# Second-layer preparation moved to earlier tiles, its first unit dealt over the last tile, and the output scatters of the first chunk sent one per unit

## The chip, the cores and the metric

The kernel runs on one NeuronCore of a Trainium2 chip. A core has a matrix engine (TensorE, PE in the profile, its weight loads PEld), a vector engine (DVE), an activation engine (ScalarE, ACT), a general engine (GpSimd, POOL) and a queue engine (SyncE, SP) that here only issues DMAs. Each engine runs its own list of instructions in the order in which the program wrote it; semaphores order the engines against each other. The metric is the time of one execution in microseconds of the device, from start to end.

## The reference, cut to what matters

Three stages over N = 1152 tokens of width 512: attention with 8 heads of 64 (half of the heads with a local window of 32, half with a stride of 32), a routed layer (each token goes to the one of eight experts that its gate picks), and a dense layer (each token goes through all four experts, weighted by given shares).

```
x = attention(q, k, v)                                # [1152, 512]
e_idx = argmax(x @ w_gate + modality_bias[modality])  # first layer: 8 experts, width 1024
y[mask] = gate_w[mask] * (relu(x[mask] @ w1[e]) @ w2[e])
out += p[:, e] * (relu(y @ w1b[e]) @ w2b[e])          # second layer: 4 experts, width 1024
```

All of it is in float32. The kernel makes each float32 product from three passes: an operand is split into a high part (a rounded copy, made by ACT) and a low part (the difference, made by DVE or POOL), and TensorE adds high by high, high by low and low by high.

## The kernel before

The schedule is written out by hand; the order in which the Python code calls the helpers is the order of each engine's list.

**Attention and routing** take the first 100 us or so and are not touched.

**First layer** (`moe1`, 11 tiles of 128 tokens that share an expert). It is a software pipeline over k = 0 to 11: iteration k does the first product of tile k (`mm1`, lines 1016) between the transposes of tile k-1's hidden values (`htr`, line 1023) and then the second product of tile k-1 (`mm2`, lines 1037 to 1039, four steps u = 0 to 3 of six matmuls). The iteration that multiplies tile t for the second time is thus k = t + 1. The 512 KB weight blocks come through SP into eight buffers `raw` and are split by `W.ahead`, ACT making `wh` (line 844) and DVE `wl` (line 845). After step u the function `mid` is called, and after the tile `after`; they are `first_layer_mid(t, u)` and `first_layer_start(t)`. In the last iteration, k = n = 11, there is no tile left for a first product, and `before_last` puts the products of the second layer's first unit in its place.

**Preparing the second layer's tokens.** `places()` works out, in five steps of a few small DVE instructions, where each token lies. `x2_gather(j)` is an indirect DMA from POOL's queue that fetches block j of 128 tokens (line 1095). `x2_prep(j)` has two steps: the first transposes the block on TensorE (line 1128), copies it back (ACT, line 1130), forms four sums on POOL (lines 1134 to 1137) and splits three quarters (ACT line 1141, POOL line 1142); the second splits the four sums (the same two lines, 512 wide). The table `PREP` says after which (t, u) a step is called; u = 4 stands for the call in `after`. Four blocks, the first chunk of 512 tokens, are prepared within the first layer; the five others later.

**Second layer** (`m2_unit`, 32 units: two chunks of tokens, four experts, four quarters of the width). One unit makes seven products of six matmuls each (lines 1261 to 1263) in three PSUM banks X, Y and Z, from sums of quarters in the manner of Strassen. Bank X is used four times in a row and ACT or DVE reads it in between (`hidden`, and the copies of lines 1287, 1294, 1299). Between the products the second products of the unit before are woven in (`m2_mm2`, lines 1413 to 1416). The weights of a unit come from `Pieces`, a generator of five pieces a unit: `a` (768 columns), two of `w` and two of `s` (512 columns each). Each is split by ACT (line 1180) and DVE (line 1181) when `PC.put` or `hidden` asks for it. The two `s` pieces hold sums of weights that POOL forms in place after the `a` piece has been split:

```
nc.gpsimd.tensor_tensor(a22, a22, a21, op=ALU.add)        # 1201
nc.gpsimd.tensor_tensor(a21, a11, a21, op=ALU.subtract)   # 1202
nc.gpsimd.tensor_tensor(a11, a22, a11, op=ALU.subtract)   # 1203
nc.gpsimd.tensor_tensor(a12, a12, a11, op=ALU.subtract)   # 1204
```

**Output.** When the last expert has been added to a block of 128 rows (line 1426), `scatter(j)` sends the rows to their places in the output with an indirect DMA from POOL's queue (line 1431). There are four in the first chunk, all in unit 16, and five in the second chunk, at the very end.

Of the kernel before, what the change touches and what calls it, by code (L numbers as in the profile page):

```python
# [111 lines left out]
def fused_kernel(  # L112
# [486 lines left out]
    def with_rows(y, idx, n=NTOK):  # L599

        nc.gpsimd.indirect_dma_start(  # L601
            out=y[:, DM:], out_offset=None, in_=xx[:n, :], in_offset=bass.IndirectOffsetOnAxis(ap=idx, axis=0)
        )
# [244 lines left out]
    def m1_gather(t, pool):  # L848
        g = pool.tile([P, XW], F32, name="g")
        nc.gpsimd.indirect_dma_start(  # L850
            out=g[:, :DM], out_offset=None, in_=xe, in_offset=bass.IndirectOffsetOnAxis(ap=idx16[:, t : t + 1], axis=0)
        )
        return g
# [142 lines left out]
    def moe1(mp, tiles, W, gs, pool, mid, after, before_last):  # L996
        n = len(tiles)
        xs, hs, ys = {}, {}, {}

        def xprep(k):  # L1000
            g = gs.pop(k)
            y = mp.tile([P, XW], F32, name="y", bufs=3)
            with_rows(y, idx16[:, tiles[k] : tiles[k] + 1])
            xs[k] = x_parts(g) if k else x0
            ys[k] = y
            if k + 2 < n:
                gs[k + 2] = m1_gather(tiles[k + 2], pool)

        def mm1(k, ph, kc):
            xh, xl = xs[k]  # L1010
            key = "1", tiles[k], kc
            wh, wl = W.out.pop(key)
            s = slice(P * kc, P * (kc + 1))
            for xx, ww, first, last in ((xh, wh, kc == 0, False), (xh, wl, False, False), (xl, wh, False, kc == KC - 1)):
                for i in range(2):
                    nc.tensor.matmul(ph[i], xx[:, s], ww[:, 512 * i : 512 * (i + 1)], start=first, stop=last)
            W.release(key)

        def htr(k, i, ht):
            pt = pst.tile([P, 512], F32, name="ps_a")  # L1020
            for c in range(4):
                s = slice(512 * i + P * c, 512 * i + P * (c + 1))
                nc.tensor.transpose(pt[:, P * c : P * (c + 1)], hs[k][:, s], ident)
            hh = mp.tile([P, 512], F32R, name="hh")
            hl = mp.tile([P, 512], F32R, name="hl")
            split(hh, hl, pt)
            ht.append((hh, hl))

        def mm2(k, ht, py, u):
            key = "2", tiles[k], u  # L1030
            wh, wl = W.out.pop(key)
            for i in range(2):
                kc = 2 * u + i
                hh, hl = ht[kc // 4]
                s = slice(P * (kc % 4), P * (kc % 4 + 1))
                f = slice(512 * i, 512 * (i + 1))
                nc.tensor.matmul(py, hh[:, s], wh[:, f], start=(kc == 0), stop=False)
                nc.tensor.matmul(py, hh[:, s], wl[:, f], start=False, stop=False)
                nc.tensor.matmul(py, hl[:, s], wh[:, f], start=False, stop=(kc == FC - 1))
            W.release(key)  # L1040

        xprep(0)
        xprep(1)
        W.ahead()
        for k in range(n + 1):
            ht = []
            if k == n:
                before_last(W, 0)
            if k < n:
                ph = [psb.tile([P, 512], F32, name="ps_b") for _ in range(2)]  # L1050
                mm1(k, ph, 0)
            if k > 0:
                htr(k - 1, 0, ht)
            W.ahead()
            if k == n:
                before_last(W, 1)
            if k < n:
                mm1(k, ph, 1)
            if k > 0:
                htr(k - 1, 1, ht)  # L1060
            W.ahead()
            if k < n:
                mm1(k, ph, 2)
                if 0 < k < n - 1:
                    xprep(k + 1)
                W.ahead()
                mm1(k, ph, 3)
                h = mp.tile([P, FF], F32, name="h")
                for i in range(2):
                    nc.scalar.activation(h[:, 512 * i : 512 * (i + 1)], ph[i], AF.Relu)  # L1070
                hs[k] = h
                W.ahead()
            if k > 0:
                py = psb.tile([P, 512], F32, name="ps_b")
                for u in range(4):
                    mm2(k - 1, ht, py, u)
                    if k == n and u < 2:
                        before_last(W, 2 + u)
                    mid(tiles[k - 1], u)
                    if u < 3:  # L1080
                        W.ahead()
                y = ys.pop(k - 1)
                nc.scalar.activation(y[:, :DM], py, AF.Copy, scale=y[:, DM : DM + 1])  # L1083
                t = tiles[k - 1]
                nc.scalar.dma_start(out=ye[(t + 1) * P : (t + 2) * P, :], in_=y)
                W.ahead()
                after(t)
# [231 lines left out]
    place = places()  # L1319
# [1 line left out]
    first, prep = {}, {}  # L1321

    def first_layer_start(t):
        if t >= 3:
            next(place, None)
        for j in {5: (0, 1), 6: (2,), 7: (3,)}.get(t, ()):
            x2_gather(j)
        prep_step(t, 4)


    PREP = {(6, 2): 0, (7, 0): 0, (7, 1): 1, (7, 4): 1, (8, 0): 2, (8, 3): 2, (8, 4): 3, (9, 0): 3}

    def prep_step(t, u):
        j = PREP.get((t, u))
        if j is not None:
# [2 lines left out]
            PC.put((u + 1) // 2)  # L1338

    def first_layer_mid(t, u):  # L1340
        if t >= 3 and u == 1:
            next(place, None)
        prep_step(t, u)

# [7 lines left out]
    def second_layer_start(W, n):  # L1352

        if n == 0:
            m2_bank.extend(psb.tile([P, 512], F32, name="ps_b") for _ in range(3))
            first["u"] = m2_unit(0, first_tmp)
            PC.put(2)
        for _ in range((2, 2, 1, 2)[n]):
            next(first["u"])


# [40 lines left out]
    for q in range(2):  # L1402
        t = xh2.rearrange("p q c t -> p (q c t)"), xl2.rearrange("p q c t -> p (q c t)")
        HT.append([x[:, NH * q : NH * (q + 1)].rearrange("p (f t h o) -> p f t h o", f=2, h=2, o=HP) for x in t])

    def m2_mm2(u, i, fh, cols=slice(0, DM)):

        c, e, fb = units2[u]
        hh, hl = (h[:, fh, i].rearrange("p h o -> p (h o)") for h in h_of(u))
        wh, wl = (w[:, 512 * fh : 512 * (fh + 1)][:, cols] for w in WT["w", u])  # L1410
        po = m2_acc[i][:, cols]
        part = (c, e, i) == (1, E2 - 1, CHT[1] - 1)
        nc.tensor.matmul(po, hh, wh, start=(fb == 0 and fh == 1), stop=False, skip_group_check=part)  # L1413
        nc.tensor.matmul(po, hh, wl, start=False, stop=False, skip_group_check=part)  # L1414
        last = fb == FC // 2 - 1 and fh == 0
        nc.tensor.matmul(po, hl, wh, start=False, stop=last, skip_group_check=part)  # L1416
        if last:
            j = CH0[c] + i
            if e == 0:
                rows[j] = raws[KC + i // 2][:, DM * (i % 2) : DM * (i % 2 + 1)]  # L1420
            pe = ext2[:, j, 1 + e : 2 + e]
            row = rows[j][:, cols]
            if e == 0:
                nc.vector.tensor_scalar(row, po, pe, None, op0=ALU.mult)
            else:
                nc.vector.scalar_tensor_tensor(row, po, pe, row, op0=ALU.mult, op1=ALU.add)  # L1426
            if e == E2 - 1 and cols.stop == DM:
                scatter(j)

    def scatter(j):  # L1430
        nc.gpsimd.indirect_dma_start(  # L1431
            out=out,
            out_offset=bass.IndirectOffsetOnAxis(ap=oid[:, j : j + 1], axis=0),
            in_=rows[j],
            in_offset=None,
        )

    def second_groups(u):
        return [(u, i, fh) for fh in (1, 0) for i in range(CHT[units2[u][0]])]
# [4 lines left out]
        return raws[RAW - 1][:, HX * "abd".index(k) :][:, :HX]  # L1444

    lag = second_groups(0)

    def second(n):
        for _ in range(min(n, len(lag))):
            m2_mm2(*lag.pop(0))  # L1450
# [4 lines left out]
    for u in range(1, NU2):  # L1455
        slots = (1, 1, 1, 1, 2, 1, len(lag))
        for k, _ in enumerate(m2_unit(u, tmp)):
            second(slots[k])
        for x in second_groups(u):
            (late if u >= NU2 - 3 and x[1] >= 3 else lag).append(x)  # L1460
        if u == 2:
            for j in range(CHT[0], NR):
                x2_gather(j)
        if u >= 4:
            j, step = divmod(u - 4, 2)
            if j < CHT[1]:
                j += CHT[0]
                next(prep.setdefault(j, x2_late(j)), None)
# [112 lines left out]
```

## Time and profile before

| | us |
|---|---|
| median of three runs | 650.41 |
| lowest and highest of them | 647.19, 650.89 |
| the profiled execution | 645.77 |
| its span, first to last instruction | 644.0 |
| TensorE busy | 599.5 (93%) |
| VectorE busy | 416.2 (65%) |
| ScalarE busy | 351.3 (55%) |
| GpSimd busy | 251.6 (39%) |

The mean granted clock of TensorE over the span is 0.974 of its full speed. The shares are means over stages that differ: where an engine waits, and for whom, has to be read from the stretch itself.

### The profile page before, as it was taken

To read this page: it belongs to the slowest core of one execution; us is meant where nothing else is said; L and a number is where in the kernel's file an instruction comes from. 1 tells how busy PE (TensorE), PEld (TensorE's weight loads), DVE (VectorE), ACT (ScalarE), POOL (GpSimd) and SP (SyncE) were. 2 spreads that over 40 slices of the span, in tenths; PEclk is the share of its full clock that TensorE was granted. 3 is DMA by queue.
4 is the path that set the end of the run, shared out by engine and by line. 5 is a ranking of instruction groups with operands and counts; after the bars stand their busy time and mean duration, and the time that the engine had idled before them with its cause. 6 is when DMAs were issued, how large, how long until landed. Compare 5 with 4: busy or idle time off the path is not lost. (4 is left out here: it accounts for less than half of the span.)

```text
span 644.0 us, 10407 instructions
## 1 busy us (share of the span) xinstructions
PE 599.5 (93%) x3620; PEld 501.8 (78%) x3620; DVE 416.2 (65%) x738; ACT 351.3 (55%) x690; POOL 251.6 (39%) x309
## 2 busy tenths in 40 slices
PE   5798889999999969999999999979999999999993
PEld 3464437888887758998898989968989988998883
DVE  3455569989988876567677586645566567557531
ACT  2245259889988865456656665524444544444410
POOL 9301242113157973356657665232132112311102
PEclk9988889999999999999999999998999999999998
DMA  8975921542579553344231323132231123121001
GB/s 189 200 196 167 314 63 51 164 154 75 166 264 365 158 183 130 131 149 131 67 130 67 131 67 131 66 115 81 97 101 66 67 75 122 65 66 67 1 18 65
DMA packets 35345, 79.13 MB, mean 123 GB/s; under 512 B 6520, under 2 KB 9856, under 8 KB 34904
## 3 DMA queue, kind: packets, MB, share of 16 engines
q1 hardware_dynamic: 29912, 65.75, 32.0%
q0 software_dynamic: 2784, 7.95, 4.1%
q10 hardware_dynamic: 2592, 4.72, 2.0%
q8 instruction: 30, 0.49, 0.3%
q14 instruction: 27, 0.22, 0.1%
HBM read 98.49 MB, written 9.28 MB: 167 GB/s over the span
## 5 line engine op out<-in xcount | busy, mean ns | idle before, releaser
L1181 DVE TENSOR_TENSOR wl<-raw,wh 128x512 fp32r<-128x512 f32 (+1 forms) x160 | 123.2, 772 | 60.9 <-ACT wh L1180 59.9
L845 DVE TENSOR_TENSOR wl<-raw,wh 128x1024 fp32r<-128x1024 f32 x88 | 108.5, 1264 | 18.4 <-ACT wh L844 18.3
L1180 ACT CAST wh<-raw 128x512 fp32r<-128x512 f32 (+1 forms) x160 | 102.8, 663 | 12.1 <-POOL raw L1204 12.0
L1201 POOL TENSOR_TENSOR raw<-raw 128x256 f32<-128x256 f32 x32 | 24.3, 760 | 192.7 <-DVE wl L1181 192.6
L844 ACT CAST wh<-raw 128x1024 fp32r<-128x1024 f32 x88 | 90.1, 1054 | 11.3 <-ACT y L1083 3.6
L1273 DVE TENSOR_TENSOR m2t<-ps_b,raw 128x320 f32<-128x320 f32 (+1 forms) x93 | 42.1, 453 | 42.3 <-PE ps_b L1263 41.2
L1261 PE MATMUL ps_b<-xh,wh 128*128 128x256 f32 x224 | 64.2, 287 | 4.6 <-ACT xh L1287 4.6
L1263 PE MATMUL ps_b<-xh,wl 128*128 128x256 f32 x224 | 63.5, 284 | 0.0
L1262 PE MATMUL ps_b<-xl,wh 128*128 128x256 f32 x224 | 63.5, 284 | 0.0
L1261 PE MATMUL ps_b<-x,wh 128*128 128x320 f32 x160 | 50.2, 314 | 5.4 <-DVE m2t L1273 5.4
L1261 PEld LDWEIGHTS ps_b<-xh,wh 128*128 128x128 f32 x224 | 42.7, 191 | 9.9 <-ACT xh L1287 4.8
L1262 PE MATMUL ps_b<-x,wh 128*128 128x320 f32 x160 | 49.8, 311 | 0.0
L1263 PE MATMUL ps_b<-x,wl 128*128 128x320 f32 x160 | 49.7, 311 | 0.0
L1262 PEld LDWEIGHTS ps_b<-xl,wh 128*128 128x128 f32 x224 | 42.7, 191 | 4.3
L1276 ACT ACTIVATE hh2b<-m2t 128x256 fp32r<-128x256 f32 (+1 forms) x45 | 20.0, 444 | 43.0 <-DVE m2t L1273 41.0
L1276 ACT ACTIVATE hh2a<-m2t 128x256 fp32r<-128x256 f32 (+1 forms) x42 | 18.7, 445 | 44.5 <-DVE m2t L1273 44.5
L1263 PEld LDWEIGHTS ps_b<-xh,wl 128*128 128x128 f32 x224 | 42.8, 191 | 0.0
L601 POOL DMA_INDIRECT y<-xx,idx x11 | 13.9, 1267 | 68.1 <-DMA ye<-y 43.3
L1261 PEld LDWEIGHTS ps_b<-x,wh 128*128 128x128 f32 x160 | 30.4, 190 | 9.3 <-DVE m2t L1273 5.9
L1414 PE MATMUL ps_b<-wl,hh2a 128*128 128x512 f32 x90 | 35.8, 397 | 0.0
L1413 PE MATMUL ps_b<-wh,hh2a 128*128 128x512 f32 x90 | 35.8, 397 | 0.0
L1416 PE MATMUL ps_b<-wh,hl2a 128*128 128x512 f32 x90 | 35.5, 395 | 0.0
(270 smaller groups left out, 1555.7 us busy)
## 6 DMA issues: line engine op xcount, KB each, us to landing
raw<-in_w1a_dram SPq DMA_DIRECT2D x48, 512.0 KB
raw<-in_w2a_dram SPq DMA_DIRECT2D x48, 512.0 KB
raw<-in_w1b_dram SPq DMA_DIRECT2D x32, 512.0 KB
raw<-in_w2b_dram SPq DMA_DIRECT2D x32, 512.0 KB
ye<-y ACTq DMA_DIRECT2D x11, 260.0 KB
kvl<-in_kvl_dram SPq DMA_DIRECT2D x2, 792.0 KB
ye<-he ACTq DMA_DIRECT2D x5, 260.0 KB
kvl<-in_kvl_dram SPq DMA_DIRECT2D x2, 614.0 KB
```

Source lines behind the costliest of these rows:

```text
L844: nc.scalar.copy(dst_h, src)
L845: nc.vector.tensor_tensor(dst_l, src, dst_h.bitcast(F32), op=ALU.subtract)
L1180: return (lambda: nc.scalar.copy(h[:, s], src[:, s])), (lambda: nc.vector.tensor_tensor(l[:, s], src[:, s], h[:, s].bitcast(F32), op=ALU.s ...
L1181: lambda: nc.vector.tensor_tensor(l[:, s], src[:, s], h[:, s].bitcast(F32), op=ALU.subtract)
L1261: nc.tensor.matmul(ph, wh[:, kc], xh, start=first and kc == 0, stop=False, skip_group_check=True)
L1262: nc.tensor.matmul(ph, wh[:, kc], xl, start=False, stop=False, skip_group_check=True)
L1263: nc.tensor.matmul(ph, wl[:, kc], xh, start=False, stop=kc == 1, skip_group_check=True)
L1273: nc.vector.tensor_tensor(t, a, b, op=ALU.add)
L1276: nc.scalar.activation(h, a, AF.Relu)
L1413: nc.tensor.matmul(po, hh, wh, start=(fb == 0 and fh == 1), stop=False, skip_group_check=part)
L1414: nc.tensor.matmul(po, hh, wl, start=False, stop=False, skip_group_check=part)
L1416: nc.tensor.matmul(po, hl, wh, start=False, stop=last, skip_group_check=part)
```

## The change

It has four parts. The steps of `places()` are called twice a tile from tile 1 on, in place of twice from tile 3 on. The gathers go out after tiles 3, 4, 5 and 7 in place of 5, 5, 6 and 7, and the preparation's steps follow after (4, 2) to (9, 0) in place of (6, 2) to (9, 0). The first unit's seven products are dealt 2, 0, 2, 2, 1 over five places of the last tile in place of 2, 2, 1, 2 over four, and the two pieces that were split ahead of its first product are now asked for at the third place. The scatters of the first chunk are kept in a list `done`, of which one is sent after each unit.

```diff
                 for u in range(4):
                     mm2(k - 1, ht, py, u)
-                    if k == n and u < 2:
+                    if k == n and u < 3:
                         before_last(W, 2 + u)
                     mid(tiles[k - 1], u)
...
     def first_layer_start(t):
-        if t >= 3:
-            next(place, None)
-        for j in {5: (0, 1), 6: (2,), 7: (3,)}.get(t, ()):
+        for j in {3: (0,), 4: (1,), 5: (2,), 7: (3,)}.get(t, ()):
             x2_gather(j)
         prep_step(t, 4)
...
-    PREP = {(6, 2): 0, (7, 0): 0, (7, 1): 1, (7, 4): 1, (8, 0): 2, (8, 3): 2, (8, 4): 3, (9, 0): 3}
+    PREP = {(4, 2): 0, (5, 0): 0, (5, 2): 1, (6, 0): 1, (6, 2): 2, (7, 0): 2, (8, 2): 3, (9, 0): 3}
...
     def first_layer_mid(t, u):
-        if t >= 3 and u == 1:
+        if t >= 1 and u in (1, 3):
             next(place, None)
         prep_step(t, u)
...
             first["u"] = m2_unit(0, first_tmp)
+        if n == 2:
             PC.put(2)
-        for _ in range((2, 2, 1, 2)[n]):
+        for _ in range((2, 0, 2, 2, 1)[n]):
             next(first["u"])
...
             if e == E2 - 1 and cols.stop == DM:
-                scatter(j)
+                done.append(j)
+                if c:
+                    scatter(done.pop(0))
...
     lag = second_groups(0)
+    done = []
...
         for k, _ in enumerate(m2_unit(u, tmp)):
             second(slots[k])
+        if done:
+            scatter(done.pop(0))
```

No instruction is added or taken away but for how the POOL list groups its scatters; instructions change places in the lists of PE, DVE, ACT and POOL, and SP's list of loads is the same.

First, ACT's list around the end of tile 7 (iteration k = 8), where the second step of one block and the first of the next are near each other. The numbers behind `raw`, `ye` and the like tell buffers apart; `COPY g` is line 1130, a first step's copy, and `xh_1640<-ye` is a second step. Before:

```order
L1141 CAST xh_1640<-ye_2625 128x8x64
L844 CAST wh<-raw_82 128x1024
L1130 COPY g<-ps_b 128x512
L1141 CAST xh_1640<-g 128x2x64 x3
L844 CAST wh<-raw_83 128x1024
L844 CAST wh<-raw_76 128x1024
L1083 ACTIVATE y<-ps_b,y 128x512
L1085 DMA ye<-y 128x520
L844 CAST wh<-raw_77 128x1024
L1141 CAST xh_1640<-ye_2765 128x8x64
L844 CAST hh<-ps_a 128x512
```

And now, at the end of tile 5 (iteration k = 6), where these two steps of the same two blocks stand:

```order
L1141 CAST xh_1640<-ye_2363 128x8x64
L844 CAST wh<-raw_82 128x1024
L844 CAST wh<-raw_83 128x1024
L1130 COPY g<-ps_b 128x512
L1141 CAST xh_1640<-g 128x2x64 x3
L844 CAST wh<-raw_76 128x1024
L1083 ACTIVATE y<-ps_b,y 128x512
L1085 DMA ye<-y 128x520
L844 CAST wh<-raw_77 128x1024
L844 CAST hh<-ps_a 128x512
L844 CAST wh<-raw_78 128x1024
L844 CAST hh<-ps_a 128x512
```

The second step of the second block, which stood six rows behind its first step, now comes thirteen rows behind it (the last one is not shown), at the end of the next tile.

Second, ACT's list at the start of the last iteration of the first layer. `raw_76` 128x512 are the `s` pieces of unit 0, `raw_77` its `w` pieces, `raw_78` and `raw_79` those of unit 1; `hh<-ps_a` splits the last tile's hidden values for its second product. Before:

```order
L1083 ACTIVATE y<-ps_b,y 128x512
L1085 DMA ye<-y 128x520
L1180 CAST wh<-raw_76 128x512 x2
L1287 COPY xh<-ps_b 128x256
L1180 CAST wh<-raw_78 128x768
L1276 ACTIVATE hh2a<-ye_3105 128x4x64
L844 CAST hh<-ps_a 128x512
L1294 COPY xl<-ps_b 128x256
```

And now:

```order
L1083 ACTIVATE y<-ps_b,y 128x512
L1085 DMA ye<-y 128x520
L1287 COPY xh<-ps_b 128x256
L1180 CAST wh<-raw_76 128x512
L1276 ACTIVATE hh2a<-ye_3097 128x4x64
L844 CAST hh<-ps_a 128x512 x2
L1180 CAST wh<-raw_76 128x512
L1180 CAST wh<-raw_78 128x768
L1294 COPY xl<-ps_b 128x256
```

The copy of line 1287 moved ahead of the two `s` pieces; one of them still stands ahead of the two `hh`, the other moved behind them.

Third, POOL's list in units 16 and 17, with the scatters (lines 1431 before, 1432 now) among the sums of lines 1201 to 1204. Before:

```order
L1431 DMA out_dram<-raw_80,oid 1152x512 x2
L1431 DMA out_dram<-raw_81,oid 1152x512
L1201 TENSOR_TENSOR raw_76<-raw_76 128x256
L1202 TENSOR_TENSOR raw_76<-raw_76 128x256
L1203 TENSOR_TENSOR raw_76<-raw_76 128x256
L1204 TENSOR_TENSOR raw_76<-raw_76 128x256
L1431 DMA out_dram<-raw_81,oid 1152x512
L1201 TENSOR_TENSOR raw_78<-raw_78 128x256
```

And now, the first of four such places:

```order
L1201 TENSOR_TENSOR raw_76<-raw_76 128x256
L1202 TENSOR_TENSOR raw_76<-raw_76 128x256
L1203 TENSOR_TENSOR raw_76<-raw_76 128x256
L1204 TENSOR_TENSOR raw_76<-raw_76 128x256
L1432 DMA out_dram<-raw_80,oid 1152x512
L1201 TENSOR_TENSOR raw_78<-raw_78 128x256
```

The three scatters that stood ahead of the sums for unit 18 stand behind them, one behind the sums of each unit.

## Rows read from the trace of the kernel before

**Rows 1.** Page, part 1: busy time of the engines, share of the span, instructions.

```profile
PE 599.5 (93%) x3620; PEld 501.8 (78%) x3620; DVE 416.2 (65%) x738; ACT 351.3 (55%) x690; POOL 251.6 (39%) x309
```

**Rows 2.** Waits of TensorE from 90 us on: total, times, longest (us).

```profile
PE ps_b L1261 <- DVE m2t L1273: 5.4, 1, 5.4
PE ps_b L1261 <- ACT xh L1287: 4.6, 1, 4.6
PE ps_a L858 <- DVE hl L845: 1.8, 1, 1.8
```

**Rows 3.** Windows k=6 to 11: length; PE, PEld, DVE, ACT, POOL busy; clock; DMA; GB/s.

```profile
165.24:177.65 12.41, 12.41 (x61) 10.20 (x60) 11.79 (x15) 11.11 (x14) 2.56 (x3) 1.00 0.70 214
177.65:190.50 12.85, 12.85 (x65) 10.58 (x64) 11.42 (x12) 11.21 (x17) 5.79 (x7) 1.00 0.78 248
190.50:203.58 13.08, 13.06 (x65) 10.51 (x64) 11.10 (x10) 12.59 (x21) 9.80 (x11) 1.00 1.01 381
203.58:218.80 15.22, 13.44 (x69) 10.82 (x68) 12.44 (x12) 12.47 (x19) 13.78 (x17) 1.00 0.49 161
218.80:232.10 13.30, 12.63 (x60) 9.76 (x59) 10.05 (x10) 10.64 (x18) 13.14 (x16) 1.00 0.95 330
232.10:249.73 17.63, 13.04 (x75) 11.79 (x74) 12.43 (x20) 9.00 (x19) 9.23 (x10) 0.90 0.25 82
```

**Rows 4.** Windows: after the wait in k = 11; unit 17, after its wait; unit 19.

```profile
238.70:242.20 3.50, 3.50 (x17) 3.50 (x18) 3.30 (x6) 2.94 (x7) 1.66 (x2) 0.55 0.52 157
421.97:442.42 20.45, 15.01 (x74) 13.22 (x73) 9.17 (x17) 6.39 (x13) 7.70 (x10) 0.83 0.34 125
436.14:439.95 3.81, 3.81 (x13) 3.52 (x14) 2.08 (x4) 1.60 (x3) 0.00 (x0) 0.52 0.64 229
455.54:468.62 13.08, 13.08 (x73) 11.79 (x72) 7.19 (x13) 5.93 (x12) 3.06 (x5) 1.00 0.24 82
```

**Rows 5.** Timeline of ACT: start, length (us), instruction [idle before it, releaser].

```profile
199.78 0.64 ACT L1141 CAST xh<-ye 128x512 fp32r<-128x512 f32 x1
...
201.24 0.60 ACT L1130 COPY g<-ps_b 128x512 f32<-128x512 f32 x1
201.88 0.70 ACT L1141 CAST xh<-g 128x128 fp32r<-128x128 f32 x3
...
208.73 0.62 ACT L1141 CAST xh<-ye 128x512 fp32r<-128x512 f32 x1 [2.15 <-POOL ye L1137]
...
237.24 1.14 ACT L1180 CAST wh<-raw 128x512 fp32r<-128x512 f32 x2 [4.25 <-POOL raw L1204]
...
434.34 1.14 ACT L1180 CAST wh<-raw 128x512 fp32r<-128x512 f32 x2 [6.08 <-POOL raw L1204]
```

**Rows 6.** Timeline of POOL, same columns: a gather, sums, and scatters.

```profile
195.56 0.99 POOL L1095 DMA_INDIRECT g<-ye,cidx  x1
...
233.30 1.18 POOL L1201 TENSOR_TENSOR raw<-raw 128x256 f32<-128x256 f32 x1
...
236.48 0.72 POOL L1204 TENSOR_TENSOR raw<-raw 128x256 f32<-128x256 f32 x1
...
426.71 0.97 POOL L1431 DMA_INDIRECT out_dram<-raw,oid  x1 [5.55 <-DVE hl2b L1281]
430.19 0.96 POOL L1431 DMA_INDIRECT out_dram<-raw,oid  x1 [2.50 <-issue]
...
433.59 0.72 POOL L1204 TENSOR_TENSOR raw<-raw 128x256 f32<-128x256 f32 x1
```

**Rows 7.** Line 1431 over the span: its scatters' time to landing.

```profile
DMA to landing us min/median/max: 2.7/2.7/5.8
```

**Rows 8.** Line 1095 over the span: its gathers' time to landing.

```profile
DMA to landing us min/median/max: 3.3/4.5/6.4
```

**Rows 9.** Timeline of PE: the first block's transposes, in iteration k = 7.

```profile
188.68 0.60 PE L1128 MATMUL ps_b<-mk,g 128*128 128x128 f32 x4
```

**Rows 10.** Line 1136 over the span: ns min/median/max, first and last start.

```profile
L1136 POOL TENSOR_TENSOR ye<-g,ye x4: 458/1326/1400, 191.3 to 227.3; 128x128 f32<-128x128 f32 x4
```

## Prediction

> **What bounds the kernel now.** The page's busy times come first: TensorE works for 599.5 of 644.0 us [rows 1], so the end is set by TensorE's list of work, and a change that moves instructions can only win back TensorE's holes or make new ones. The second view is the list of TensorE's waits from 90 us on. It has only three large entries: 5.4, 4.6 and 1.8 us [rows 2]. The third is the windows, which say what each hole really cost, since a hole is not only idle time: after the waits of 4.6 and 5.4 us TensorE went on at its lower level of 1.2 GHz, with a granted clock of 0.55 over 3.50 us and of 0.52 over 3.81 us [rows 4], where it stands at 1.00 otherwise. After the 1.8 us wait the clock stayed at 1.00 (k = 9 in [rows 3]). The last view is the timelines of ACT and POOL, which say who was late. Both large holes end the same way: ACT's cast of the `s` pieces waits for POOL's last sum, 4.25 us once and 6.08 us once [rows 5], and everything queued behind that cast on ACT waits too, TensorE's banks among it.
>
> Why POOL was late differs. At 230 us it is still busy with the fourth block's preparation: 13.14 us of the 13.30 of k = 10 [rows 3], so that the four sums run from 233.30 to 237.20 [rows 6]. At 430 us it stands still: a scatter waits until the one before has landed (2.50 us idle ahead of the one at 430.19), and the sums for unit 18 are queued behind the third scatter and end at 434.31 [rows 6].
>
> The profiled execution took 645.77 us, 1.77 more than its span, and is 4.6 us under the median of 650.41. I make the sum on the profile and take it off the median, since the holes sit in the program's order and should be in every run.
>
> **The scatters.** Unit 19, which makes the same products as unit 17 and the same number of second products, takes 13.08 us, and unit 17 takes 20.45 [rows 4]. The difference of 7.4 us is the price of the scatters: 5.4 us of idle time [rows 2] and 3.81 x (1 - 0.52) = 1.8 us of half clock [rows 4]. In the new list one scatter stands behind the sums of each unit. It needs about 1 us of POOL [rows 6] and lands after 2.7 to 5.8 us [rows 7]; the next is sent 13 us later, so no scatter waits for another, and POOL has work for only 3.06 us of such a unit [rows 4]. The rows in `raw` that they read are written again when unit 20 ends the second chunk's first expert; the last of the four goes out after unit 19, more than 5.8 us before that. I put the new cost at nothing: it is covered by POOL's free 10 us. **Gain 7.4 us.**
>
> **The preparation.** An iteration without a block takes 12.41 us, one with a block's transposes 12.85, so these cost 0.44 wherever they stand [rows 3]. By that measure k = 8 with one block lost 13.08 - 12.85 = 0.2 us, k = 9 with two lost 15.22 - 13.29 = 1.9, and k = 10, which has neither a block nor the four transposes of a next tile, lost 13.30 - 11.97 = 1.3 [rows 3]. Together 3.4 us are there to be won. The large piece is a second step on ACT that waits 2.15 us for POOL's sums [rows 5], because it was called three steps of `mm2` after its first step; the split of the hidden values behind it is late, and TensorE waits the 1.8 us [rows 2]. In the new list each second step comes a whole first product later, as it did for the first block in k = 7 and 8, where no such wait shows. So that is gone.
>
> What is added: ACT needs 0.64 + 0.60 + 0.70 = 1.9 us for a block [rows 5]. In an iteration without one it is busy for 11.11 of 12.41 us, and a part of the rest is its own DMA issue [rows 3]. So ACT falls behind by something like half a microsecond in each of k = 6, 7 and 8, which now carry blocks 1 and 2 and the ends of 0 to 2. VectorE is no better off with 11.79 of 12.41 [rows 3]. The nearest row is k = 8 of before, with one second and one first step in it: 0.2 us lost. The far end is k = 9 with 1.9. I take 0.3 for each of the three, 0.9 in all, since the steps now stand as in k = 8; the ends are 0 and 5.7. **Net gain 2.5 us.**
>
> The gathers have to be priced too, because they are queued on POOL behind the block before. In k = 7 the gather behind block 0's work went out at 195.56, 17.9 us after the iteration's start [rows 6]; landing takes 4.5 us in the middle and 6.4 at worst [rows 8], so the data is there after 22.4 to 24.3 us. The transposes that want it come now one iteration later, at 12.85 + (188.68 - 177.65) = 23.9 us [rows 3, 9]. That leaves 1.5 us in the middle case; before, the gather had longer. I put it at nothing, and its failure among the rivals.
>
> `places()` moves two tiles ahead, a few small DVE instructions against a DVE that is as full there; nothing queues behind them but splits that are a tile ahead of their use. I take nothing.
>
> **The last tile.** Iteration k = 11 took 17.63 us, of which TensorE was busy 13.04, so 4.6 were idle [rows 3]; 3.50 x (1 - 0.55) = 1.6 were lost to the clock [rows 4]. 6.2 us could be won. Two things change. The fourth block's first step comes two steps of `mm2` earlier and no block precedes it closely, so POOL, busy for 13.14 us of k = 10, should be free by the end of it: the sums need 3.9 us (233.30 to 237.20) [rows 6] and can start once the `a` piece is split, shortly before the iteration begins. I estimate that they end some 2.5 us after its start, not 5.1 as before. And the copy that lets TensorE go on (line 1287) no longer stands behind the `s` casts. But one `s` cast still stands ahead of the two `hh` splits, which the last tile's second product needs, and that product comes up right after the first two products and the transposes, some 2 us into the iteration, where before two more products stood in front of it. So a wait takes the place of the old one: the cast at about 2.5 us, the two splits behind it, and TensorE idle for some 2 us. Also products five and six now stand back to back on bank X, and the sixth has to wait until DVE has read the bank; before, a step of `mm2` lay between. Bounds: nothing, if POOL is early enough, and the 6.2 us of before, if it isn't. I take 2.8, under the middle, since the copy is out of the way and POOL has less ahead of it; that is short of the 4.6 us idle after which the clock fell, and not far above the 1.8 us after which it did not. **Net gain 3.4 us.**
>
> **Sum.** 7.4 + 2.5 + 3.4 = 13.3 us. The profiled execution would go to 632.5 us, the median to **637.1 us**.
>
> **A rule to weigh.** POOL's sum of line 1136, always the same size, took 458 ns at its fastest and 1326 ns in the middle of four [rows 10]: something shuts POOL out for most of a microsecond. The Trainium skill, page "SBUF — State Buffer", section "SBUF: two separate sides", has a cause: VectorE with two inputs in SBUF and GpSimd reading SBUF take a port pair that they share as an exclusive lock, for the whole instruction. The two levels agree with it. It speaks against this change, which sets every block's sums beside a VectorE that is busy 11 of 12.4 us: its result here is the late gather, the second rival.
>
> **The rivals.**
> - *The last tile keeps its hole.* If POOL's sums still end 5 us into k = 11, the `s` cast holds the `hh` splits as it held the copy, and the 17.63 us remain. For it speaks that ACT's list still has that cast ahead of the splits; against it POOL's lighter load. 637.1 + 3.4 = 640.5 us.
> - *The gathers come late.* If three of a block's four sums take 1326 ns in place of 458 [rows 10], the next gather goes out 2.6 us later, and blocks 1 and 2 wait 1.1 us in the middle case, 3.0 us with the longest landing; 2 to 6 us for both, 639 to 643, in the middle 641 us. Against it: in k = 7 the sums were mostly fast, and a late block also gives ACT time to catch up.
> - *No new hole at all.* All of 7.4 + 3.4 + 6.2 = 17.0 us is won: 633.4 us.
> - *The scatters still hold POOL,* because one behind the sums of its own unit stands ahead of those of the next and has to wait for something not seen here: 637.1 + 7.4 = 644.5 us. The landings in [rows 7] speak against it.
> - *Slower.* ACT and VectorE are so full in k = 5 to 10 that spreading the blocks makes every one of these six iterations lose what k = 9 and 10 lost together, 3.2 us, in place of 0.9 in all: 637.1 + 19.2 - 0.9 = 655.4 us. It decides from (13.3 + 0.9) / 6 = 2.4 us an iteration on. Against it, k = 8 lost 0.2 with a comparable load.
>
> **How the numbers follow.** Chances: the forecast 0.58, the kept hole 0.14, late gathers 0.12, no new hole 0.10, scatters 0.03, slower 0.03. For the range I take both ends of the new waits: 633.4 with none, less 2 us for the spread of the runs (647.19 was the lowest) makes 631; the kept hole and most of the late gathers lie below 642.5. What is left out is the last two rivals, the longest gathers, and chance. One per cent, 6.5 us, is about what a measurement here can tell from no change: faster means under 643.9 us. The first, second and fourth case and nearly all of the third lie there, 0.92; 0.05 fall within one per cent, and 0.03 lie above.
>
> **What would show it.** Unit 17 should take 13.1 us at a clock of 1.00, with one POOL scatter after each of units 16 to 19 and no wait for landing. Iterations k = 9 and 10 should take about 12.9 and 12.0 us, k = 6 to 8 up to 13.2, with no ACT wait for line 1137. k = 11 should take some 14 us, with ACT's wait for line 1204 under 2 us. The prediction is wrong if TensorE waits at line 1128 in k = 6 or 7, at line 1037 in k = 11 for 4 us or more, or if splits of weights come late in k = 5 to 8.

## The result, and the profile after

The changed kernel takes 640.12 us (median of 4 runs, 637.80 to 642.66), the kernel before 649.79 beside it (4 runs, 647.19 to 650.89). The ratio is 0.9857, with an interval of 0.9829 to 0.9884: faster by 1.4%, 9.7 us where 13.3 were forecast. The profiled execution took 639.82 us, its span is 637.9.

The page of the changed kernel, part 1, as in [rows 1]:

```profile
PE 596.5 (94%) x3620; PEld 499.2 (78%) x3620; DVE 415.1 (65%) x738; ACT 351.0 (55%) x690; POOL 252.7 (40%) x309
```

Its list of TensorE's waits, as in [rows 2]:

```profile
PE ps_b L1128 <- DMA g<-ye,cidx: 3.5, 1, 3.5
PE ps_b L1037 <- ACT hh L844: 1.5, 1, 1.5
PE ps_a L1412 <- DVE raw L1425: 0.6, 1, 0.6
PE ps_b L1261 <- DVE xh L1273: 0.5, 1, 0.5
PE ps_b L1261 <- ACT raw L1294: 0.4, 1, 0.4
```

All three waits of [rows 2] are gone, and a new one of 3.5 us stands at the top: TensorE waits at line 1128 for a gather, which the prediction had named as a sign of failure. The windows of the changed kernel say where that is; columns as in [rows 3], k = 6 to 11, then unit 1 to 15 in one row, then unit 17, and last the stretch behind the 3.5 us wait:

```profile
167.08:180.18 13.10, 13.08 (x65) 10.52 (x64) 11.11 (x10) 12.53 (x20) 11.06 (x12) 1.00 0.67 223
180.18:197.80 17.62, 14.10 (x65) 11.11 (x64) 12.41 (x13) 13.45 (x21) 15.93 (x18) 0.94 0.75 249
197.80:210.82 13.02, 13.02 (x62) 10.67 (x60) 11.09 (x10) 11.66 (x16) 7.28 (x8) 0.95 0.86 260
210.82:223.68 12.86, 12.86 (x65) 10.59 (x64) 12.42 (x13) 11.32 (x18) 5.37 (x5) 1.00 0.67 224
223.68:235.65 11.97, 11.97 (x58) 9.80 (x57) 9.14 (x9) 9.05 (x14) 6.52 (x10) 1.00 0.88 322
235.65:250.07 14.42, 12.23 (x76) 10.40 (x75) 9.30 (x17) 8.77 (x18) 6.14 (x7) 1.00 0.27 92
250.07:411.48 161.41, 161.00 (x1011) 144.03 (x1010) 109.88 (x192) 92.02 (x221) 93.83 (x130) 1.00 0.33 112
423.21:436.29 13.08, 13.08 (x73) 11.80 (x72) 9.00 (x17) 6.29 (x13) 5.59 (x7) 1.00 0.38 137
194.98:202.44 7.46, 7.46 (x32) 6.12 (x33) 3.64 (x4) 5.66 (x10) 5.03 (x11) 0.77 0.89 325
```

Against [rows 3, 4], unit 17 went from 20.45 to 13.08 us, k = 11 from 17.63 to 14.42, and k = 9 and 10 from 15.22 and 13.30 to 12.86 and 11.97. But k = 7 takes 17.62, where up to 13.2 were expected, and its wait is followed by 7.46 us at a clock of 0.77.

The timeline of POOL in the changed kernel, first around that gather, then the first two scatters (as in [rows 6]):

```profile
177.10 2.09 POOL L1142 TENSOR_TENSOR xl<-ye,xh 128x512 fp32r<-128x512 f32 x1 [1.11 <-ACT xh L1141]
179.13 1.19 POOL L1124 COPY ext<-g 128x8 f32<-128x8 f32 x1
180.27 1.18 POOL L1125 CAST oid<-g 128x1 int32<-128x1 f32 x1
181.41 1.46 POOL L1134 TENSOR_TENSOR ye<-g 128x128 f32<-128x128 f32 x1
182.95 0.47 POOL L1135 TENSOR_TENSOR ye<-g,ye 128x128 f32<-128x128 f32 x1
183.49 1.45 POOL L1136 TENSOR_TENSOR ye<-g,ye 128x128 f32<-128x128 f32 x1
184.91 0.46 POOL L1137 TENSOR_TENSOR ye<-g 128x128 f32<-128x128 f32 x1
185.33 3.27 POOL L1142 TENSOR_TENSOR xl<-g,xh 128x128 fp32r<-128x128 f32 x3
188.75 1.00 POOL L1095 DMA_INDIRECT g<-ye,cidx  x1 [0.15 <-PE ps_b L1039]
...
426.95 1.28 POOL L1432 DMA_INDIRECT out_dram<-raw,oid  x1 [0.15 <-issue]
...
438.58 1.00 POOL L1432 DMA_INDIRECT out_dram<-raw,oid  x1 [0.16 <-issue]
```

and TensorE's timeline behind that gather, the row that answers to [rows 9]:

```profile
194.98 0.66 PE L1128 MATMUL ps_b<-mk,g 128*128 128x128 f32 x4 [3.52 <-DMA g<-ye,cidx]
```

The four scatters of the first chunk go out right behind the sums of their unit, 0.15 us after the last, and none of them waits for another's landing; they land 2.7 to 3.0 us after issue. The five of the second chunk still wait for each other, as in the kernel before. TensorE's last product ends at 628.2 and VectorE has added the last rows by 628.7, but the last scatter goes out at 632.61: some 4 us at the end of the kernel that are not set by TensorE's list and that its list of waits can't show.

The gather of block 2 goes out at 188.75, 21.7 us behind the start of k = 6 (167.08), the iteration that was to cover it, because POOL first ends block 0's second step (177.10) and does the whole of block 1's first.

TensorE does the same work in every kernel here, so the stretches between its start times make a ledger. "k = 2 to 10" runs from the first product of k = 2 to that of k = 11, and all of the changed places but the scatters lie in the first three columns (us, worked out from start times in the traces; medians from the runs, each with its ratio to the kernel before of the same set of runs):

| kernel | k = 2 to 10 | k = 11 | units 1 to 15 | unit 17 | median (runs) | ratio to before |
|---|---|---|---|---|---|---|
| before | 116.47 | 17.63 | 160.52 | 20.45 | 649.79 | |
| changed | 118.62 | 14.42 | 161.41 | 13.08 | 640.12 (4) | 0.9857 [0.9829, 0.9884] |
| scatters alone | 116.56 | 17.78 | 160.52 | 13.08 | 641.24 (6) | 0.9887 [0.9859, 0.9915] |
| preparation alone | 118.62 | 15.15 | 160.50 | 21.20 | 647.54 (12) | 0.9982 [0.9960, 1.0005] |
| dealing alone | 116.44 | 18.44 | 160.48 | 20.57 | 648.85 (12) | 1.0003 [0.9979, 1.0027] |
| changed, gathers ahead | 113.56 | 14.22 | 161.35 | 13.09 | 637.36 (5) | 0.9837 [0.9811, 0.9862] |
| changed, again | 116.11 | 14.76 | 160.91 | 13.09 | 638.88 (6) | 0.9861 [0.9836, 0.9886] |
| changed, `s` behind `hh` | 118.93 | 13.16 | 162.10 | 13.09 | 640.63 (6) | 0.9865 [0.9834, 0.9895] |
| gathers ahead, old dealing | 113.57 | 15.81 | 160.48 | 13.08 | 635.83 (6) | 0.9808 [0.9779, 0.9837] |
| gathers ahead, `s` behind `hh` | 113.58 | 13.59 | 162.04 | 13.08 | 636.93 (6) | 0.9825 [0.9801, 0.9849] |
| changed, hh2b moved | 115.97 | 14.70 | 160.46 | 13.08 | 639.56 (4) | 0.9887 [0.9830, 0.9943] |
| gathers ahead, hh2b moved | 113.74 | 16.90 | 160.46 | 13.08 | 636.85 (4) | 0.9830 [0.9770, 0.9891] |
| the same, old dealing | 113.59 | 15.21 | 160.49 | 13.09 | 635.37 (4) | 0.9807 [0.9764, 0.9850] |
| gathers ahead, old dealing, again | 113.59 | 16.71 | 160.47 | 13.09 | 634.80 (4) | 0.9800 [0.9757, 0.9843] |

The two profiles of before and after differ by 5.95 us, less than the medians do. The first reason lies ahead of the change: the start of k = 2, after attention and routing, which no kernel here touches, falls at 115.63 in the profile of before, at 117.03 in that of after, and between 113.97 and 119.61 in the others. Without that 1.4 the pair gives 7.35. The second is the gather's wait: 3.5 us in this profile, 2.3 in that of the same kernel taken again, whose row gives -0.36 -2.87 +0.39 -7.36 = -10.2 us.

### The profile page after: what moved, and what is told of

The parts are those of the page before. It is cut to its first block, busy times and chain, and to the rows that moved or that the text cites. A ratio compares the mean times of both kernels' runs of the same rounds, so it can differ in the third digit from the quotient of the medians.

```text
span 637.9 us, 10401 instructions
## 1 busy us (share of the span) xinstructions
PE 596.5 (94%) x3620; PEld 499.2 (78%) x3620; DVE 415.1 (65%) x738; ACT 351.0 (55%) x690; POOL 252.7 (40%) x309
## 4 chain that ended last, share of the span: by engine, by line
PE 77%; ACT 3%; DMA 2%; DVE 1%; issue 1%; POOL 1%; POOLq 0%; ACTq 0%; DVEq 0%
PE ps_b L1261 9%; PE ps_b L1262 9%; PE ps_b L1263 9%; PE ps_b L1016 8%; PE ps_b L1413 7%; PE ps_b L1412 7%; PE ps_b L1415 7%; PE ps_a L1412 4%; PE ps_a L1413 3%; PE ps_a L1415 3%; PE ps_b L1039 3%; PE ps_b L1038 2%; PE ps_b L1037 2%; ACT wh L844 2%; PE ps_a L1023 1%
## 5 line engine op out<-in xcount | busy, mean ns | idle before, releaser
L1037 PE MATMUL ps_b<-wh,hh 128*128 128x512 f32 x88 | 35.1, 399 | 1.5 <-ACT hh L844 1.5
L1412 PE MATMUL ps_b<-wh,hh2b 128*128 128x512 f32 x90 | 35.5, 394 | 0.0
```

## The experiments

The first four tell apart the parts of the change and the cause of the new wait.

**Scatters alone.** The kernel before, with the list of scatters:

```diff
             if e == E2 - 1 and cols.stop == DM:
-                scatter(j)
+                done.append(j)
+                if c:
+                    scatter(done.pop(0))
...
+    done = []
...
+        if done:
+            scatter(done.pop(0))
```

> The kernel before with the list of scatters alone (one of the first chunk's after each of units 16 to 19). Theory: unit 17 falls from 20.45 to 13.1 us and nothing else changes, 7.4 us faster than before (ratio about 0.989); as the changed kernel won about 9.7 us, the scatters are then most of it. Rival: part of the 7.4 us was not the scatters but a late start that unit 17 inherits, and unit 17 keeps 2 us or more of its hole: 5 us faster or less.

641.24 us, 0.9887: with 7.37 us off unit 17 it brings most of what the whole change brings. Nothing else in its ledger moves by more than 0.15 us.

**Preparation alone.** The kernel before, with the new places of `places()`, gathers and steps:

```diff
-        for j in {5: (0, 1), 6: (2,), 7: (3,)}.get(t, ()):
+        for j in {3: (0,), 4: (1,), 5: (2,), 7: (3,)}.get(t, ()):
...
-    PREP = {(6, 2): 0, (7, 0): 0, (7, 1): 1, (7, 4): 1, (8, 0): 2, (8, 3): 2, (8, 4): 3, (9, 0): 3}
+    PREP = {(4, 2): 0, (5, 0): 0, (5, 2): 1, (6, 0): 1, (6, 2): 2, (7, 0): 2, (8, 2): 3, (9, 0): 3}
...
-        if t >= 3 and u == 1:
+        if t >= 1 and u in (1, 3):
             next(place, None)
```

> The kernel before with places, gathers and preparation moved ahead, old dealing of the first unit and old scatters. Theory: iterations k = 5 to 10 are slower together by about 2 us than before, because the transposes of block 2 wait for their gather (3.5 us idle and a stretch at half clock) while k = 9 and 10 win 3.4; in k = 11 POOL's sums end about 2.6 us sooner, so that its wait falls from 4.6 to some 2 us and the clock stays up, 4 us won; 2 us faster than before in sum (ratio 0.997). Rival: the shorter k = 11 came from the new dealing, not from POOL being free sooner; then k = 11 keeps its 17.6 us and this kernel is 2 us slower than before.

647.54 us, 0.9982, no difference that can be told. Its list of TensorE's waits shows why, and that the hole of k = 11 shrinks without any new dealing:

```profile
PE ps_b L1261 <- DVE m2t L1273: 6.0, 1, 6.0
PE ps_b L1128 <- DMA g<-ye,cidx: 3.5, 1, 3.5
...
PE ps_b L1261 <- ACT xh L1287: 1.9, 1, 1.9
```

The wait for the `s` casts is 1.9 us, where [rows 2] had 4.6, and k = 11 takes 15.15; the late gather gives it back in k = 7. The 6.0 is the scatters' wait in unit 17, as before.

**Dealing alone.** The kernel before, with the seven products of the first unit over five places:

```diff
-                    if k == n and u < 2:
+                    if k == n and u < 3:
...
+        if n == 2:
             PC.put(2)
-        for _ in range((2, 2, 1, 2)[n]):
+        for _ in range((2, 0, 2, 2, 1)[n]):
```

> The kernel before with the new dealing of the first unit alone. Theory: POOL is as late as before, so one s cast waits until 5.1 us into k = 11, the hh splits behind it, and TensorE waits some 3.9 us at line 1037 in place of 4.6 at line 1261: at most 1 us faster. Rival (the dealing is what shortened k = 11): k = 11 falls to 14.4 us as in the changed kernel, 3 us faster.

648.85 us, 1.0003. The wait in k = 11 only changes its line (4.3 us; the rest of the 5.0 is a wait in k = 10 that the kernel before has too):

```profile
PE ps_b L1037 <- ACT hh L844: 5.0, 2, 4.3
...
PE ps_b L1261 <- DVE xh L1273: 0.7, 1, 0.7
```

This is the rival "the last tile keeps its hole", and it is what the dealing does while POOL is late: the `hh` splits wait behind the `s` cast as the copy did, and k = 11 takes 18.44 us.

**Gathers ahead.** The changed kernel, with two gathers sent earlier, so that none stands on POOL behind the sums of the block before:

```diff
-        for j in {3: (0,), 4: (1,), 5: (2,), 7: (3,)}.get(t, ()):
+        for j in {3: (0, 1), 7: (3,)}.get(t, ()):
             x2_gather(j)
...
+        if (t, u) == (5, 1):
+            x2_gather(2)
         prep_step(t, u)
```

> The changed kernel with two gathers sent sooner: block 1's with block 0's after tile 3, block 2's after step (5, 1), so that neither is queued on POOL behind the first step of the block before. Theory: TensorE's wait of 3.5 us at line 1128 in k = 7 and the half clock behind it go, k = 7 falls from 17.6 to about 13.1 and k = 8 from 13.0 to 12.4 us, 5 us faster than the changed kernel (635 us, ratio to before 0.978). Rival: ACT and VectorE are too full in these tiles and the late gather is only where it shows; then TensorE waits elsewhere in k = 6 to 8 (lines 858, 1037) and wins 2 us or less.

637.36 us, 0.9837. The windows of k = 7 and 8 in this kernel:

```profile
180.17:193.11 12.94, 12.94 (x65) 10.52 (x64) 12.09 (x13) 12.45 (x20) 12.30 (x13) 1.00 0.76 227
193.11:205.79 12.68, 12.64 (x61) 10.13 (x60) 12.03 (x11) 12.23 (x17) 11.69 (x13) 1.00 1.02 357
```

and POOL's row of block 2's gather, which goes out 9.4 us earlier than at 188.75:

```profile
179.32 1.78 POOL L1095 DMA_INDIRECT g<-ye,cidx  x1
```

The wait at line 1128 and the half clock are gone, and k = 2 to 10 takes 113.56 us, 2.9 under the 116.47 of before and 5.06 under the changed kernel's profile. So the late gather is shown to be the cause. Its price changes from one execution to the next: the five profiles with the late gather take 115.97 to 118.93 us for k = 2 to 10, the three longer ones with half clock behind a wait of 3.5 to 3.8 us, the two shorter ones with a wait of 2.2 or 2.3 us and no half clock. In time the gain is less clear: 5 us were expected, the median is 2.8 us under the changed kernel's, 1.3 by the ratios to before, and the two intervals overlap.

The next four were to find what k = 11 could still give.

**The changed kernel again**, as the control of this set, with no edit.

> The changed kernel itself, as the measure for the three beside it and to see whether its hole in k = 7 is there in a second profile. Theory: the gather of block 2 is late because of what is queued ahead of it, in every run: TensorE waits 2 to 4 us at line 1128 in k = 7 again. Rival: the wait was an unlucky landing; then it is under 1 us this time and the kernel has a profile of about 635 us.

638.88 us, 0.9861, the result a second time. The wait at line 1128 is there again, 2.3 us long, this time without half clock behind it.

**The `s` pieces behind the `hh` splits.** The changed kernel; `PC` gives nothing out from the first place to the third, where three pieces are asked for:

```diff
+            if self.hold:
+                return nothing
...
+            PC.hold = True
         if n == 2:
-            PC.put(2)
-        for _ in range((2, 0, 2, 2, 1)[n]):
+            PC.hold = False
+            PC.put(3)
+        for _ in range((2, 0, 1, 2, 2)[n]):
```

> The changed kernel with both s pieces asked for behind the two hh splits, and the first unit dealt 2, 0, 1, 2, 2. Theory: the wait of 1.5 us at line 1037 in k = 11 came from the s cast ahead of the hh splits, and the 0.5 us from products five and six back to back; k = 11 falls from 14.4 to about 12.4 us, 2 us faster than the changed kernel. Rival: the s pieces are then late themselves, TensorE waits for them at the third product instead, and no more than 0.5 us is won.

640.63 us, 0.9865: nothing gained. The windows of k = 11 and of units 1 to 15 in this kernel say that k = 11 fell by 1.3 us against the changed kernel's first profile and units 1 to 15 gave back 0.7 of it, with a wait of 1.1 us in unit 1 for the copy of line 1294:

```profile
238.37:251.53 13.16, 12.25 (x75) 10.30 (x74) 8.84 (x16) 8.45 (x17) 5.92 (x7) 1.00 0.28 100
251.53:413.63 162.10, 161.02 (x1012) 144.00 (x1010) 109.99 (x193) 92.30 (x221) 94.04 (x130) 1.00 0.34 111
```

**Gathers ahead, old dealing.** The kernel with the gathers ahead, and the four places of before:

```diff
-                    if k == n and u < 3:
+                    if k == n and u < 2:
...
-        if n == 2:
             PC.put(2)
-        for _ in range((2, 0, 2, 2, 1)[n]):
+        for _ in range((2, 2, 1, 2)[n]):
```

> The changed kernel with the two gathers sent sooner and with the old dealing of the first unit (2, 2, 1, 2, two pieces split ahead). Theory: once the preparation is early the dealing is worth nothing: k = 11 takes 15.2 us as in the run with the moved preparation alone, units 1 to 15 together 160.5 in place of 161.4, and the time is within 0.5 us of the kernel with the gathers ahead (0.984 of before). Rival: the new dealing is worth the 3 us by which k = 11 got shorter; then this is 2 to 3 us slower than that kernel.

635.83 us, 0.9808, the best so far, 3.05 us under the changed kernel beside it. So the dealing is worth nothing that shows in the time. Its windows of k = 11 and of units 1 to 15:

```profile
231.93:247.74 15.81, 13.25 (x76) 11.67 (x75) 10.70 (x18) 8.77 (x18) 7.05 (x9) 0.89 0.27 88
247.74:408.22 160.48, 160.48 (x1011) 144.14 (x1010) 108.53 (x190) 92.23 (x220) 93.33 (x130) 1.00 0.33 112
```

**Gathers ahead and `s` behind `hh`**, both edits on the changed kernel.

> Gathers ahead, s pieces behind the hh splits, dealing 2, 0, 1, 2, 2, one scatter after a unit. Theory: the 5 us of the late gather and the 2 us of k = 11 are separate and add up: 7 us faster than the changed kernel, about 633 us, 0.976 of before. Rival: a second stage takes back what the first wins (the ring of weights or the loads come late), and it stays within 3 us of the changed kernel.

636.93 us, 0.9825: as the gathers ahead alone. The 633 us of two gains that add up did not come.

The last four ask why unit 1 is longer wherever the new dealing shortens k = 11. ACT's first write of `hh2b` (line 1276), the odd units' hidden values, comes 4.1 to 4.8 us behind the issue of the last tile's `y` in the five kernels above with the new dealing and the early preparation, and 3.0 to 3.3 in all the others so far. `hh2b` is the first buffer of a pool that is opened where the first layer's pool, with `y` in it, is closed. In the three kernels with the edit below it is taken behind ten others of that pool:

```diff
-    HT.append([m2p.tile([P, 2, max(CHT), 2, HP], F32R, name=n) for n in ("hh2b", "hl2b")])
...
     spare += [m2p.tile([P, 2 * HX], F32R, name=f"x1_{i}") for i in range(10)]
+    HT.append([m2p.tile([P, 2, max(CHT), 2, HP], F32R, name=n) for n in ("hh2b", "hl2b")])
```

**The changed kernel, hh2b moved.**

> The changed kernel with the two buffers of the odd units' hidden values (hh2b and its low part) taken behind ten others of the same pool, so that they lie in another place. Theory A: unit 1's first write of hh2b on ACT comes late because its memory held the last tile's y, which must have been sent away first; then the write, 4.5 us behind the issue of that transfer in the changed kernel, comes 2.0 to 3.0 us behind it, TensorE's 0.4 us wait for line 1294 in unit 1 goes, and the time falls by 0.4 to 1 us, at the edge of what can be told. Theory B: the write is held by something else; then it stays 4 us or more behind the issue and nothing changes.

The timeline of ACT in unit 1, first of the changed kernel:

```profile
250.99 0.33 ACTq L1085 DMA_DIRECT2D ye<-y  x1
...
255.50 0.42 ACT L1276 ACTIVATE hh2b<-m2t 128x256 fp32r<-128x256 f32 x1 [3.25 <-issue]
```

and of the kernel with `hh2b` moved:

```profile
248.98 0.33 ACTq L1085 DMA_DIRECT2D ye<-y  x1
...
250.89 0.42 ACT L1276 ACTIVATE hh2b<-m2t 128x256 fp32r<-128x256 f32 x1 [0.65 <-DVE m2t L1273]
```

The write comes 1.9 us behind the issue, TensorE's wait for line 1294 is gone, and units 1 to 15 take 160.46 us in place of 161.41. That the place in memory held the write is shown. What freed it stands in the traces' semaphores: in the changed kernel the last report that `y` has landed comes at 255.43, ACT's wait for these reports ahead of line 1276 ends at 255.45, and the write starts at 255.50. In all eleven kernels with `hh2b` in its old place the write starts 0.07 us behind that landing, also where the profile names another releaser; in the three with `hh2b` moved it starts 1.2 to 2.5 us ahead of it.

What differs among the eleven is the landing itself, 4.0 to 4.8 us behind the issue in five and 3.0 to 3.3 in six. SP issues two weight loads of 512 KB just ahead of `y`, and in all fourteen kernels `y` lands 5.1 to 5.7 us behind the second of them, whether it was issued 0.9 or 2.1 us behind it. So a last tile that ends sooner behind these loads does not have its `y` away sooner; that `y` queues behind them is argued from these times, since no run moved the loads.

The median, 639.56, can't tell a gain of that size.

**Gathers ahead, hh2b moved**, with the new dealing:

> The kernel with the gathers ahead and the new dealing, with hh2b in another place. Theory A: the write comes 2 to 3 us behind the issue of y's transfer in place of 4.4, k = 11 with units 1 to 15 takes about 175.0 us in place of 175.57, and the median is 636 to 637, as good as the old dealing. Theory B: 4.4 us, 175.6 us and 637.4 again.

Units 1 to 15 take 160.46 again, but k = 11 takes 16.90: the wait for the `hh` splits is 2.6 us in this profile, and half clock follows it. The two together take 177.36 us where 175.0 were expected. 636.85 us.

**The same with the old dealing:**

> The kernel with the gathers ahead and the old dealing, with hh2b in another place. In that kernel the write of hh2b came 3.0 us behind the issue and waited for VectorE's split of weights by the profile, so both theories expect no change: 635.8 us, between 634.5 and 637; theory A allows 0.3 us less.

635.37 us, 0.9807, and 160.49 in units 1 to 15, no change, as expected. But the reason given was wrong: the write comes 2.0 us behind the issue, 3.25 in the same kernel without the move, so here too the landing had held it, at no cost to TensorE.

**Gathers ahead and old dealing, again**, with no edit.

> The same kernel as the one with the gathers ahead and the old dealing, again, beside its variant with hh2b moved. If it is better than the changed kernel it comes out at 0.981 of before again, within 0.003; if its 635.83 was luck, at 0.984 to 0.986.

634.80 us, 0.9800: the best version stands, 2% under the kernel before.

## Why the prediction was right, and where it was not

The sign, the range and the largest term held; the sum was 3.6 us too large. That the median lies in the range is in part luck: one term came out near nothing or with the wrong sign, and the range was wide enough for it.

**Scatters: right, in mechanism and size.** 7.4 us were forecast, 7.37 came off unit 17, at a clock of 1.00, and the new scatters cost nothing: from the end of unit 17 to the end of the span it is 201.6 us before and after.

**Preparation: the step that failed is "I put it at nothing", said of the gathers.** With it came one of the prediction's own signs of being wrong, a wait at line 1128. The terms around it were right: k = 9 and 10 came out at 12.86 and 11.97, k = 6 at 13.10, no wait of ACT for line 1137 is left, and with the gathers sent ahead the forecast net gain of 2.5 us is there as 2.9. But in place of those -2.5 us the changed kernel has +2.15 in this profile, and -0.36 in the second. Three assumptions were too kind. I took the 17.9 us of k = 7 in [rows 6] for the gather's delay. POOL's timeline in the kernel before, where that block's sums and splits begin:

```profile
189.98 0.67 POOL L1134 TENSOR_TENSOR ye<-g 128x128 f32<-128x128 f32 x1 [3.29 <-ACT g L1130]
...
193.12 2.29 POOL L1142 TENSOR_TENSOR xl<-g,xh 128x128 fp32r<-128x128 f32 x3
```

There POOL had one block's work, here it first had the second step of the block before, for which it waited (1.11 us idle at 177.10), and the sums began 14.3 us into the iteration, not 12.3. From there to the gather it took 7.34 us, not 5.58. And the data came 6.2 us after issue, near the worst of [rows 8], not after 4.5. Together 2.0 + 1.8 + 1.7 = 5.5 us against a slack of 1.5; as TensorE was itself 0.5 late, 3.5 us of idle time are left. My rival of the late gathers had a part of this mechanism, slow sums, at 1.1 to 3.0 us a block. Measured, the sums made the gather 0.8 us later (3.92 us in place of 3.14), the splits of line 1142 1.0 (3.42 in place of 2.44), and the queue ahead of them, which the rival did not have, 2.0. It also left the clock out: the half clock behind the wait cost another 7.46 x (1 - 0.77) = 1.7 us. Only block 2 was hit, not block 1.

In the row of POOL's work, the sums of lines 1134 and 1136 took 1.46 and 1.45 us where those of 1135 and 1137 took 0.47 and 0.46. The Trainium skill's rule that the prediction weighed ("SBUF — State Buffer", section "SBUF: two separate sides"), an exclusive lock between VectorE with two inputs in SBUF and GpSimd, agrees with these two levels. The start and end times in the traces of before and after say more. Of the 16 sums of lines 1134 to 1137 in each, 9 and 6 began while VectorE ran a split of weights (line 845, both operands in SBUF), and every one of them ended 0.32 or 0.33 us behind the end of that split. The others took 0.46 or 0.47 us, also the four that began beside a split that reads PSUM. So POOL is shown to have been held until VectorE's split was done; no run here took these splits away.

**Last tile: the size and the new waits right, the credit in part wrong.** k = 11 took 14.42 us where "some 14" were forecast, with ACT's wait for line 1204 at 0.87 us. POOL's sums ended 2.5 us into it, at 238.15, as estimated, and TensorE waited 1.5 us at line 1037 and 0.5 for product six, where "some 2 us" stood in the forecast. I gave the credit to both POOL's earlier end and the copy's place in the new dealing. The runs divide it: the early preparation alone brings 17.63 to 15.15, the dealing alone brings nothing (18.44). With the early preparation the old dealing has 15.15 to 16.71 us in four profiles, the new one 14.22 to 16.90 in five. Of what the new one wins there, units 1 to 15 give back 0.4 to 0.9 us where `hh2b` was not moved: the wait for the landing of `y`, which no term of mine held. k = 11 and units 1 to 15 together take 175.65 to 177.18 us with the old dealing and 175.16 to 177.36 with the new one, so the two can't be told apart there. Why the medians favour the old dealing by some 1.5 us, with the gathers ahead and once more with `hh2b` moved, stays open. The ledgers of the first pair differ by 0.7 us the other way, those of the second by 1.8 us the same way, and the intervals overlap.

**The rivals.** Slower and blocked scatters are excluded by the ledger. The kept hole is what the dealing alone does. The late gathers happened, at block 2 only, while the rest of the forecast held; 641 us was given for them, 640.1 was measured, nearer than the 637.1 of the forecast.

## What to carry to other kernels

When a step is moved earlier, price the queue in front of its DMA at the new place, with what other steps put there, and not at the place where it was measured; sending a gather as soon as its addresses and data exist is cheaper than any such estimate. When several edits come together, run each alone: some three quarters of this gain (7.4 of 9.7 us) came from one of three edits, and one edit was worth nothing. Compare stretches between start times on the bounding engine, since spans carry the luck of stages that nobody touched, and look at the stage behind the one that was shortened for what it gives back.

## What the runs showed of the hardware

TensorE's clock did not follow the length of the wait alone, as I had taken it to do. I had relied on the 1.8 us wait of [rows 2], which cost no clock. In the kernel with gathers ahead, old dealing and hh2b moved, TensorE's timeline has this wait:

```profile
233.61 0.40 PE L1261 MATMUL ps_b<-xh,wh 128*128 128x256 f32 x1 [1.99 <-ACT xh L1287]
```

and the window behind it:

```profile
233.61:237.40 3.79, 3.79 (x18) 3.75 (x19) 3.35 (x7) 3.37 (x8) 1.95 (x2) 0.55 0.55 189
```

In the changed kernel with hh2b moved, TensorE's timeline, and under it the window behind the wait:

```profile
237.66 0.50 PE L1037 MATMUL ps_b<-wh,hh 128*128 128x512 f32 x1 [1.85 <-ACT hh L844]
```

```profile
237.66:242.00 4.34, 4.20 (x23) 3.43 (x24) 3.49 (x6) 3.21 (x7) 1.30 (x2) 1.00 0.27 58
```

Two waits of nearly the same length: behind the first TensorE went on near 1.2 GHz for most of 3.79 us (0.55), behind the second at 2.4 GHz. Two more say the same: in the preparation alone a wait of 1.9 us in k = 11 was followed by 0.61 over 3.83 us, in the changed kernel again one of 1.9 us by 1.00 to the end of k = 11. What decides between them stays open. A wait of 2 us can cost 1.7 us more than itself, so a forecast that leaves one standing has to hold both prices.
